# Three weight sums from VectorE to GpSimd, and a new order of turns, sums and writes around the fifth and sixth unit of a linear-attention and MLP kernel

## The chip, the core and the metric

The kernel runs on one core of a Trainium2 chip. The metric is the device time of one execution in microseconds. The core has TensorE (PE, with its weight loads shown as PEld), VectorE (DVE), ScalarE (ACT), GpSimd (POOL) and the DMA queues, most of which SyncE (SP) issues here. Each engine works through its own instructions in program order and waits on semaphores for the others.

## What is computed

The first half is a recurrence over 768 steps, for 4 batches and 8 heads of 48 channels; the second is an MLP with SiLU on its output.

```
for t in range(S):
    cur = einsum('bhd,bhe->bhde', u * k[t], v[t])
    y[t] = einsum('bhd,bhde->bhe', r[t], state + cur)
    state = w[t][..., None] * state + einsum('bhd,bhe->bhde', k[t], v[t])
x = y.transpose(0, 2, 1, 3).reshape(3072, 384)
h = x @ w_in                     # 384 -> 2048
out = (h * sigmoid(h)) @ w_out   # 2048 -> 384
```

Everything is float32.

## The kernel before

The work is cut into 12 units: 6 chunks of 128 time steps by 2 pairs of batches. The code counts them from 0, so the fourth, fifth, sixth and last unit are units 3, 4, 5 and 11. A unit has three parts, and the main loop (L1435) runs them staggered: its pass i does the attention of unit i (`mix(i)`), the second MLP layer of unit i-2 (`downs`) and the first MLP layer of unit i-1 (`ups`). `mix(i)` returns a list of groups, each a list of attention steps with a count: after a group's steps so many steps of the MLP are issued. This list is an order written out by hand, and since every engine keeps program order, it sets who runs before whom on each engine and on SP's DMA queue. Places in the text are indices into that list.

**Attention of a unit.** `turn` transposes raw w, k or r from tokens to channels (DVE, L361, two instructions, one for each batch). `product` (POOL, L410) builds the running products of w over 2, 4, 8, ... steps, levels 0 to 6. `grow_own`, `grow_keys` (POOL, L651 and L642) and `grow_queries`, `prepare` (DVE, L624 and L779) multiply these into keys and queries. `burst` (PE, L700) makes the scores of two levels, `keep_masked` (DVE, L718) and ACT (L800) keep the right blocks of them. The scores inside small blocks come another way: `block_bonus` (POOL, L493, steps 0 to 7) multiplies on untransposed data, `block_sum` (DVE, L530) reduces, `block_move` sends the sums through DRAM, `block_turn` (L563) and `block_write` (DVE, L569, one predicated copy for each half of the heads) put them into the score tile; units below 4 use `bonus_write` (L598) instead. At the end `y_state` (PE, L843 and L850) and `y_values` (L864) read the whole score tile.

**First MLP layer.** For units 0 to 2 it is a plain product (`up`, L1078). From unit 3 (`NFAST`) on, the layer is done as 20 products of weight combinations by combinations of x (`first_part`, PE at L1185), a bilinear scheme that saves multiplications. I call them by their numbers in `ORDER`: 20, 18, 14, 13, 2, 15, 4, 7, 19, 16, 1, 12, 9, 11, 3, 6, 10, 5, 8, 17. They accumulate in four PSUM banks A to D (`h1`, `h0`, `o1`, `o0`); ACT copies, SiLUs (L1209) and DVE joins (L1212) work on the banks in between. The combinations of x are DVE instructions (`sums_of_x`, steps 0 to 7, L1146 to L1166). The combinations of the weights are made once, 512 columns at a time, by `in_weight_sum` (L1124), during passes 3 and 4, on DVE or POOL; `weight_plan` names them (`q`, `n13`, `t`, `u1`, `u`, `q19`, `q9` and so on) and says what each reads and writes. Half of them overwrite blocks of `w_in_sb` that the plain products of unit 2 have read before.

**Second MLP layer.** It works the same way with 7 products (`quarter`, PE at L1328) of 192 columns. Quarters 2 to 5 use combinations of the SiLU outputs: `sums(i, m)` makes s1, s3, s2, s4 in this order on DVE (L1299) for m = 0 and 1. The seven results go through three places x, z, y in the banks `o0`, `h1`, `o1`: quarters 0, 2, 4 and 6 in x, 1 in z, 3 and 5 in y. A quarter may not go on in its place before the result that was there has been read: by ACT (L1333) after quarters 0, 2, 3 and 6, by DVE (L1336) after 1, 4 and 5. So quarter 6 waits for DVE's L1336 after quarter 4. Product 18 of the next first layer starts in bank `o1` and so waits for L1336 after quarter 5; product 17 is the last that uses `o0`.

In pass i the order on PE is: quarters of unit i-2, the first `burst`, products of unit i-1 with the second `burst` among them (between 11 and 3), `turn_apart`, `y_state`, `y_values`, `update`.

Of the kernel before, what the change touches and what calls it, by code (L numbers as in the profile page):

```python
# [38 lines left out]
def kernel(  # L39
# [921 lines left out]
    def mix(i):  # L961
# [12 lines left out]
        def turns(j):  # L974
            return [*at(j <= NPAIR, *both(turn, j, "w"), (product, j, 0)), *both(turn, j, "k")]

        def start(j):
            return [*at(j <= NPAIR, *products_of(j, *range(1, NL))), (grow_own, j, 1)]

# [6 lines left out]
        if i < NPAIR:  # L986
# [8 lines left out]
                      [(prepare, i, 5), (make_block_mask,), (bonus_spread, i)],  # L995
                      [(burst, i, 5), (keep_level, i, 5, 0), (keep_level, i, 6, 0), (go_on, i, 6), (bonus_write, i, (0,)), (keep_level, i, 5, 1), (keep_level, i, 6, 1), (bonus_write, i, (1,))], *end]
            groups = list(zip(groups, (1, 1, 0, 2, 1, 1, 1, 1, 1, 2, 2, 1, 1)))
        else:
            j = i - 1
            if i <= NPAIR:  # L1000
# [18 lines left out]
                          ([(block_write, i, 0), *at(i == NPAIR, *both(turn, i + 1, "w"))], 1),  # L1019
                          ([*end[0], *at(i == NPAIR, *products_of(i + 1, *range(NL)))], 2), (end[1], 0)]  # L1020
            else:
# [6 lines left out]
                groups = [([*both(turn, i, "r"), (grow_own, i, 0), (x_out, j, nc.sync), *loads("w", 0, 1)], 2),  # L1028
                          ([*at(j >= NPAIR, (add_update, j)), *start(i), *bonus_steps(i, 4), (x_in, j, nc.sync), *loads("w", 2, 3), (reverse_v, i)], 1),
                          ([*keys_2, *loads("k", 0, 1)], 1),  # L1030
                          ([*keys_3, (sums_of_x, j, 0, 1), *loads("k", 2)], 1),
                          ([(sums_of_x, j, 2), *bonus_steps(i, 6, 7), (sums_of_x, j, 3, 4, 5, 6), *loads("k", 3)], 2),
                          ([(burst, i, 3), *sum_steps(i, 3), (keep_level, i, 3), *sum_steps(i, 4)], 2),
                          ([(block_move, i, False), *at(ahead, (load_rk, i + 1, (0, 1)), (turn, i + 1, 0, "w"))], 1),
                          ([*loads("r", 0)], 1),
                          ([(block_move, i, True), *at(ahead, (turn, i + 1, 1, "w"), *products_of(i + 1, 0, 1, 2)), (keep_level, i, 4)], 2),
                          ([(go_on, i, 4), *at(ahead, *products_of(i + 1, 3, 4, 5, 6))], 1),
# [5 lines left out]
                          ([*loads("r", 3)], 1),  # L1043
                          ([(burst, i, 5), (keep_level, i, 5, 0), (keep_level, i, 6, 0), *at(ahead, *bonus_steps(i + 1, 0)), (go_on, i, 6), (block_turn, i), (block_write, i, 1)], 2),
                          ([(keep_level, i, 5, 1), (keep_level, i, 6, 1)], 1),
                          ([(block_write, i, 0)], 1),
                          ([*at(ahead, *bonus_steps(i + 1, 1, 2, 3)), ], 2),
# [238 lines left out]

    def sums(i, m):

# [8 lines left out]
        for out, one, two, op in ((s1, lower[1], upper[1], ALU.add), (s3, lower[0], lower[1], ALU.subtract),  # L1297
                                  (s2, s1, lower[0], ALU.subtract), (s4, upper[0], s2, ALU.subtract)):
            nc.vector.tensor_tensor(out=out, in0=one, in1=two, op=op)  # L1299
# [3 lines left out]
    def quarter(i, which):  # L1303
# [16 lines left out]
        if which in (0, 1, 3):  # L1320
            if i < NFAST - 1:
                pool, tag = (ps, "p_h") if place == "z" else (second[0], "p_o")
                sum_of[i, place] = pool.tile([128, DH], F32, name=tag, bufs=2)
            else:
                sum_of[i, place] = kept[{"x": "o0", "y": "o1", "z": "h1"}[place]][:, 0:DH]
        p = sum_of[i, place]
# [160 lines left out]
```

## Time and profile before

| | |
|---|---|
| median of 3 runs | 574.52 us (574.39 to 574.62) |
| the profiled execution | 573.2 us |
| its span, first to last instruction | 571.4 us |
| outside the span | 1.8 us |
| PE, DVE, POOL, ACT busy | 555.4, 481.7, 394.3, 270.8 us |
| granted TensorE clock | 1.0 in every slice |

A row of the timeline has the start, the duration, engine, line, operation, output and inputs, form and count; a bracket at its end is the idle time of the engine before the row and what ended it. Neighbouring instructions of one line are merged into a row with their count. Times are in microseconds from the span's start. The passes begin on PE with quarter 0: pass 4 at 169.97, pass 5 at 214.83, pass 6 at 260.57, pass 7 at 303.00, pass 11 at 471.39; the last quarters begin at 549.93.

### The profile page before, as it was taken

The numbers are of one execution on the slowest core, as the hardware profiler recorded it, in microseconds if no ns is written. First come the engines' busy times: TensorE is split into PE (matmuls) and PEld (weight loads), VectorE is DVE, ScalarE is ACT, GpSimd is POOL, SyncE is SP. The second block draws the span as 40 slices with busy tenths as digits, with TensorE's granted clock in tenths as the row PEclk, the third lists the DMA queues.
The fourth block names the chain that finished last, engine by engine and source line by source line (L and its number), as shares of the span: only waits on it lengthen the run. The fifth ranks groups of instructions, "written<-read, shape, count | busy, mean of one in ns | idle before, by whom it ended". The sixth has DMA issues, their size and how long they took to land.

```text
span 571.4 us, 18874 instructions
## 1 busy us (share of the span) xinstructions
PE 555.4 (97%) x7782; PEld 517.3 (91%) x7782; DVE 481.7 (84%) x748; ACT 270.8 (47%) x604; POOL 394.3 (69%) x447
## 2 busy tenths in 40 slices
PE   8989999999999999799999999999999999999997
PEld 8767776698889889799999999999999999999997
DVE  7979798998999999989989989989989889782250
ACT  5679695442451273274274274274274272271320
POOL 5998778537879999696696696696696696600000
PEclk9999999999999999999999999999999999999999
DMA  9955876345355365364465454465555452102000
GB/s 224 311 106 148 238 224 128 47 69 108 89 87 96 77 112 96 60 129 89 93 109 91 101 103 91 94 108 93 109 88 95 104 96 61 38 5 56 29 9 21
DMA packets 206485, 57.59 MB, mean 101 GB/s; under 512 B 186048, under 2 KB 198208, under 8 KB 206400
## 3 DMA queue, kind: packets, MB, share of 16 engines
q1 hardware_dynamic: 203712, 54.23, 46.1%
q10 hardware_dynamic: 2688, 2.16, 1.5%
q8 instruction: 61, 1.00, 0.8%
q14 instruction: 24, 0.20, 0.1%
HBM read 47.14 MB, written 9.18 MB: 99 GB/s over the span
## 4 chain that ended last, share of the span: by engine, by line
PE 73%; DVE 11%; POOL 4%; DMA 4%; SPq 3%; issue 3%; ACT 1%; DVEq 0%; POOLq 0%
PE p_o L1328 25%; PE p_o L1185 15%; PE p_h L1185 10%; PE p_h L1078 5%; PE p_h L1328 4%; PE p_m L1267 4%; PE p_sc L700 2%; PE p_m L864 2%; SPq L127 2%; POOL tk L642 2%; DVE score L718 2%; PE p_m L843 1%; DVE tr L624 1%; PE p_m L700 1%; DMA tokens_w<-in_w_dram 1%
## 5 line engine op out<-in xcount | busy, mean ns | idle before, releaser
L642 POOL TENSOR_TENSOR tk<-tk,tw 128x256 f32<-128x256 f32 x112 | 92.6, 846 | 7.8 <-DVE tw L410 3.8
L1328 PE MATMUL p_o<-own,temps 128*128 128x192 f32 x528 | 88.1, 327 | 0.2 <-DVE temps L1299 0.2
L1328 PEld LDWEIGHTS p_o<-own,temps 128*128 128x128 f32 x528 | 86.0, 190 | 0.5 <-DVE temps L1299 0.5
L1185 PE MATMUL p_o<-xt,w_in_sb 128*64 128x128 f32 x1152 | 72.1, 273 | 0.7 <-POOL w_in_sb L1124 0.7
L1078 PE MATMUL p_h<-xt,w_in_sb 128*128 128x256 f32 x288 | 66.1, 384 | 1.7 <-POOL w_in_sb L260 1.6
L1185 PEld LDWEIGHTS p_o<-xt,w_in_sb 128*64 128x64 f32 x1152 | 64.7, 137 | 0.9 <-POOL w_in_sb L1124 0.9
L1328 PE MATMUL p_o<-w_out_sb,gt 128*128 128x192 f32 x340 | 60.1, 330 | 4.1 <-DVE ob L1336 3.4
L1078 PEld LDWEIGHTS p_h<-xt,w_in_sb 128*128 128x128 f32 x288 | 53.6, 190 | 9.9 <-POOL w_in_sb L260 2.4
L410 POOL TENSOR_TENSOR tw<-tw 128x256 f32<-128x256 f32 (+6 forms) x71 | 39.6, 558 | 33.0 <-DVE tw L361 29.4
L1328 PEld LDWEIGHTS p_o<-w_out_sb,gt 128*128 128x128 f32 x340 | 55.2, 190 | 5.6 <-DVE ob L1336 4.0
L493 POOL TENSOR_TENSOR ruk<-tokens_rk 128x384 f32<-128x384 f32 x48 | 53.0, 1124 | 4.4 <-DMA tokens_rk<-in_k_dram 4.4
L624 DVE TENSOR_TENSOR tr<-tr,tw 128x512 f32<-128x512 f32 x57 | 51.6, 905 | 0.7
L1333 ACT COPY partial<-p_o 128x192 f32<-128x192 f32 x33 | 10.5, 319 | 77.2 <-PE p_o L1328 77.2
L1299 DVE TENSOR_TENSOR temps<-gt 128x512 f32<-128x512 f32 (+1 forms) x48 | 44.3, 961 | 0.0
L651 POOL TENSOR_TENSOR tk<-tk,tw 128x256 f32<-128x256 f32 x32 | 24.7, 806 | 27.5 <-DVE tk L361 27.5
L612 ACT COPY tk<-tk 128x256 f32<-128x256 f32 x52 | 20.9, 402 | 36.6 <-POOL tk L642 29.4
L1209 ACT ACTIVATE gt<-p_o 128x512 f32<-128x512 f32 x45 | 26.1, 602 | 25.1 <-PE p_o L1185 25.1
L1333 ACT COPY ob<-p_o 128x192 f32<-128x192 f32 x11 | 3.5, 319 | 61.2 <-PE p_o L1328 61.2
L718 DVE COPY_PREDICATED score<-mask,p_sc 128x512 f32<-128x512 int8 x42 | 31.2, 799 | 0.9 <-PE p_sc L700 0.8
L1328 PE MATMUL p_o<-w_out_sb,temps 128*128 128x192 f32 x176 | 30.4, 326 | 0.0
L1328 PE MATMUL p_h<-w_out_sb,gt 128*128 128x192 f32 x168 | 29.1, 326 | 0.0
L493 POOL TENSOR_TENSOR spare<-tokens_rk 128x384 f32<-128x384 f32 x24 | 28.6, 1204 | 0.6
(247 smaller groups left out, 1315.3 us busy)
## 6 DMA issues: line engine op xcount, KB each, us to landing
w_out_sb<-in_moe_w_in_dram SPq DMA_DIRECT2D x6, 768.0 KB, 7.5
turned<-yt SPq DMA_DIRECT2D x18, 192.0 KB, 2.6
xt<-turned SPq DMA_DIRECT2D x9, 384.0 KB, 3.4
w_out_sb<-in_moe_w_out_dram SPq DMA_DIRECT2D x4, 768.0 KB, 5.4
own<-in_moe_w_out_dram SPq DMA_DIRECT2D x4, 768.0 KB, 5.9
tokens_w<-in_w_dram SPq DMA_DIRECT2D x8, 384.0 KB, 4.4
tokens_rk<-in_r_dram SPq DMA_DIRECT2D x7, 384.0 KB, 4.7
tokens_rk<-in_k_dram SPq DMA_DIRECT2D x7, 384.0 KB, 5.9
```

What stands on the lines that cost most here:

```text
L410: engine.tensor_tensor(out=up, in0=t[:, :, 0::2], in1=t[:, :, 1::2], op=ALU.mult)
L493: mul = lambda out, one, two: nc.gpsimd.tensor_tensor(out=out, in0=one, in1=two, op=ALU.mult)
L624: nc.vector.tensor_tensor(out=odd, in0=odd, in1=tw[i][l][:, :, 0::2][:, :, :, None].to_broadcast([128, Q, L >> (l + 1), c]), op=ALU.mult)
L642: nc.gpsimd.tensor_tensor(out=out, in0=have, in1=odd_products(i, l, b, *blocks), op=ALU.mult)
L651: nc.gpsimd.tensor_tensor(out=have, in0=have, in1=odd_products(i, l, b, [2, NP * ni]), op=ALU.mult)
L718: nc.vector.copy_predicated(out=dst, mask=masks[l][:, :, None].to_broadcast([128, NB, NP, ni, c]), data=sc[e].rearrange("p (b q) (i c) -> ...
L1078: nc.tensor.matmul(p_h[:, a, :], lhsT=w_in_sb[:, c, f * 128:(f + 1) * 128], rhs=xt[i][:, c, :], start=(a == 0 and c == 0), stop=(a == 1 an ...
L1185: nc.tensor.matmul(p[h:h + PD, q, :], lhsT=left[:, f:f + PD], rhs=right, start=first and q == 0, stop=q == 3, skip_group_check=True)
L1209: nc.scalar.activation(out=g(f, t), in_=have, func=AF.Silu)
L1267: nc.tensor.matmul(po[i, b], lhsT=gt[i, f // 2][:, f % 2, b * L:(b + 1) * L], rhs=w_out_sb[:, f, :], start=(f == 0), stop=(f == FC - 1))
L1299: nc.vector.tensor_tensor(out=out, in0=one, in1=two, op=op)
L1328: nc.tensor.matmul(p, lhsT=left(f), rhs=right[:, f, :], start=which in (0, 1, 3) and f == 0, stop=f == FH - 1, skip_group_check=True)
```

## The change

No instruction is added or taken away; instructions change their engine or their place in the order, and one PSUM place changes its bank.

1. Weight sums. `q`, `n13`, `t` (POOL) go from place 11 of pass 3 to place 10, ahead of `block_bonus` 0 to 3 of unit 4. `u1`, `u`, `q19`, which DVE made in pass 4 (places 5 and 7), are made by POOL at place 11 of pass 3, behind `block_bonus` 0 to 3.
2. Turns. The two turns of w of unit 4 go from the end of pass 3 to place 10 of pass 3, ahead of the `bonus_write`s. In pass 5 the first turn of w of unit 6 goes from place 6 to place 8, next to the second.
3. Products of w. Levels 1 to 6 of unit 5 go from the end of pass 4 (place 19) into pass 5 (place 1, behind `grow_own` level 0). Level 0 stays.
4. Sums. Of `sums(3, 1)` only s1 and s2 stay at the end of pass 4; s3 and s4 go into pass 5, behind the turns of r. `sums_of_x` 0 and 1 go from place 3 to place 4, behind quarter 4 with its L1336, in passes 5 and 11.
5. Writes. In pass 5 `block_write` 1 goes from place 16 to place 18, directly ahead of `block_write` 0 and behind product 10 with its join.
6. The last unit's quarter 0 (and with it 2, 4 and 6) accumulates in a bank of `p_sc` instead of `o0`.

```diff
         def turns(j):
-            return [*at(j <= NPAIR, *both(turn, j, "w"), (product, j, 0)), *both(turn, j, "k")]
+            return [*at(j <= NPAIR, (product, j, 0)), *both(turn, j, "k")]
         def start(j):
-            return [*at(j <= NPAIR, *products_of(j, *range(1, NL))), (grow_own, j, 1)]
+            return [*at(j <= NPAIR + 1, *products_of(j, *range(1, NL))), (grow_own, j, 1)]
...
-    ... (go_on, i, 6), (bonus_write, i, (0,)), ...
+    ... (go_on, i, 6), *at(i == NPAIR - 1, *both(turn, i + 1, "w")), (bonus_write, i, (0,)), ...
...
-    ([*end[0], *at(i == NPAIR, *products_of(i + 1, *range(NL)))], 2), (end[1], 0)]
+    ([*end[0], *at(i == NPAIR, *products_of(i + 1, 0))], 2), (end[1], 0)]
...
-    groups = [([*both(turn, i, "r"), (grow_own, i, 0), ...
+    groups = [([*both(turn, i, "r"), *at(j == NPAIR, (sums, j - 1, 1, (1, 3))), (grow_own, i, 0), ...
...
-    ([*keys_3, (sums_of_x, j, 0, 1), *loads("k", 2)], 1),
-    ([(sums_of_x, j, 2), *bonus_steps(i, 6, 7), ...
+    ([*keys_3, *at(NPAIR + 1 < i < len(units) - 1, (sums_of_x, j, 0, 1)), *loads("k", 2)], 1),
+    ([*at(i in (NPAIR + 1, len(units) - 1), (sums_of_x, j, 0, 1)), (sums_of_x, j, 2), *bonus_steps(i, 6, 7), ...
...
-    ([(block_move, i, False), *at(ahead, (load_rk, i + 1, (0, 1)), (turn, i + 1, 0, "w"))], 1),
+    ([(block_move, i, False), *at(ahead, (load_rk, i + 1, (0, 1))), *at(ahead and i > NPAIR + 1, (turn, i + 1, 0, "w"))], 1),
...
-    ([(block_move, i, True), *at(ahead, (turn, i + 1, 1, "w"), ...
+    ([(block_move, i, True), *at(i == NPAIR + 1, (turn, i + 1, 0, "w")), *at(ahead, (turn, i + 1, 1, "w"), ...
...
-    ... (block_turn, i), (block_write, i, 1)], 2),
+    ... (block_turn, i), *at(i > NPAIR + 1, (block_write, i, 1))], 2),
...
-    ([(block_write, i, 0)], 1),
+    ([*at(i == NPAIR + 1, (block_write, i, 1)), (block_write, i, 0)], 1),
...
-    def sums(i, m):
+    def sums(i, m, which=range(4)):
...
-    sum_of[i, place] = kept[...][:, 0:DH]
+    sum_of[i, place] = bank("p_sc", DH) if i == len(units) - 1 and which == 0 else kept[...][:, 0:DH]
...
-    made[-1].append((sums, i, 1))
+    made[-1].append((sums, i, 1, range(4) if i > NFAST else (0, 2)))
...
-    (8, nc.vector, ("q12a", "q12")), (11, nc.gpsimd, ("q", "n13", "t"))):
+    (8, nc.vector, ("q12a", "q12")), (10, nc.gpsimd, ("q", "n13", "t")), (11, nc.gpsimd, ("u1", "u", "q19"))):
...
-    for place, engine, names in ((5, nc.vector, ("u1", "u")), (7, nc.vector, ("q19",)), (5, nc.gpsimd, ("q7",)),
+    for place, engine, names in ((5, nc.gpsimd, ("q7",)),
```

More of the change, by code (lines that the diff above doesn't have):

```diff
@@ L995, in mix @@
                       [(prepare, i, 5), (make_block_mask,), (bonus_spread, i)],
-                      [(burst, i, 5), (keep_level, i, 5, 0), (keep_level, i, 6, 0), (go_on, i, 6), (bonus_write, i, (0,)), (keep_level, i, 5, 1), (keep_level, i, 6, 1), (bonus_write, i, (1,))], *end]
+                      [(burst, i, 5), (keep_level, i, 5, 0), (keep_level, i, 6, 0), (go_on, i, 6), *at(i == NPAIR - 1, *both(turn, i + 1, "w")), (bonus_write, i, (0,)), (keep_level, i, 5, 1), (keep_level, i, 6, 1), (bonus_write, i, (1,))], *end]
             groups = list(zip(groups, (1, 1, 0, 2, 1, 1, 1, 1, 1, 2, 2, 1, 1)))
@@ L1043, in mix @@
                           ([*loads("r", 3)], 1),
-                          ([(burst, i, 5), (keep_level, i, 5, 0), (keep_level, i, 6, 0), *at(ahead, *bonus_steps(i + 1, 0)), (go_on, i, 6), (block_turn, i), (block_write, i, 1)], 2),
+                          ([(burst, i, 5), (keep_level, i, 5, 0), (keep_level, i, 6, 0), *at(ahead, *bonus_steps(i + 1, 0)), (go_on, i, 6), (block_turn, i), *at(i > NPAIR + 1, (block_write, i, 1))], 2),
                           ([(keep_level, i, 5, 1), (keep_level, i, 6, 1)], 1),
-                          ([(block_write, i, 0)], 1),
+                          ([*at(i == NPAIR + 1, (block_write, i, 1)), (block_write, i, 0)], 1),
                           ([*at(ahead, *bonus_steps(i + 1, 1, 2, 3)), ], 2),
@@ L1296, in sums @@
             s1, s2, s3, s4 = (quarters[:, x, 2 * m:2 * m + 2, :] for x in range(4))
-        for out, one, two, op in ((s1, lower[1], upper[1], ALU.add), (s3, lower[0], lower[1], ALU.subtract),
-                                  (s2, s1, lower[0], ALU.subtract), (s4, upper[0], s2, ALU.subtract)):
+        made = ((s1, lower[1], upper[1], ALU.add), (s3, lower[0], lower[1], ALU.subtract),
+                (s2, s1, lower[0], ALU.subtract), (s4, upper[0], s2, ALU.subtract))
+        for out, one, two, op in (made[x] for x in which):
             nc.vector.tensor_tensor(out=out, in0=one, in1=two, op=op)
@@ L1324, in quarter @@
             else:
-                sum_of[i, place] = kept[{"x": "o0", "y": "o1", "z": "h1"}[place]][:, 0:DH]
+                sum_of[i, place] = bank("p_sc", DH) if i == len(units) - 1 and which == 0 else kept[{"x": "o0", "y": "o1", "z": "h1"}[place]][:, 0:DH]
         p = sum_of[i, place]
```

6 lines of the change are left out of this document (3 added, 3 removed).

## The prediction

> **What bounds the kernel now.** I read the passes first, as stretches of the span: length, then busy time of PE, its weight loads, DVE, ACT and POOL.
>
> ```profile
> 169.97:214.83 44.86, 43.04 (x690) 41.37 (x688) 43.72 (x67) 18.38 (x43) 43.92 (x46) 1.00 0.51 94
> 214.83:260.57 45.74, 42.77 (x693) 41.59 (x689) 42.43 (x62) 20.57 (x52) 39.85 (x46) 1.00 0.50 92
> 260.57:303.00 42.43, 42.43 (x689) 41.54 (x689) 39.03 (x61) 20.50 (x52) 32.80 (x37) 1.00 0.52 97
> 430.30:471.39 41.09, 41.09 (x641) 40.23 (x641) 37.68 (x60) 19.05 (x49) 31.85 (x37) 1.00 0.53 100
> 471.39:513.22 41.83, 41.36 (x641) 40.20 (x641) 36.31 (x60) 17.85 (x42) 20.57 (x25) 1.00 0.15 35
> ```
>
> Pass 6 is filled by PE: 42.43 of 42.43 us, at full clock. Pass 4 takes 2.43 us more and pass 5 3.31 us more; pass 11 takes 0.74 us more than pass 10, which has the same work on PE. In pass 4 DVE and POOL are busy for all but 1 us. So the most there is to win is 2.43 + 3.31 + 0.74, and something at the end. The timeline of PE shows the places (start, duration, ..., idle before it and its releaser).
>
> ```profile
> 196.21 1.09 PE L1185 MATMUL p_o<-gt,in_sum 128*64 128x128 f32 x16 [0.96 <-DVE p_o L1212]
> 202.36 1.09 PE L1185 MATMUL p_o<-xt,w_in_sb 128*64 128x128 f32 x16 [0.69 <-POOL w_in_sb L1124]
> 227.93 2.76 PE L1328 MATMUL p_o<-w_out_sb,temps 128*128 128x192 f32 x16
> 233.66 2.87 PE L1328 MATMUL p_o<-w_out_sb,gt 128*128 128x192 f32 x16 [2.97 <-DVE ob L1336]
> ```
>
> The first is product 4, waiting for the join after 13, which DVE does late; the second is product 9, waiting for its weights `q9` from POOL; the last is quarter 6 in pass 5, waiting for DVE to read quarter 4's result. That one wait is nearly all that pass 5 loses.
>
> **Part by part.** *The sums of x behind the read of quarter 4* (change 4).
>
> ```profile
> 231.69 0.80 DVE L1146 TENSOR_TENSOR xt<-xt 128x256 f32<-128x256 f32 x1
> 233.25 0.36 DVE L1336 TENSOR_TENSOR ob<-p_o,partial 128x192 f32<-128x192 f32 x1
> ```
>
> DVE works through its order up to this read; `sums_of_x` 0 and 1 take it from 231.69 to 233.25, so L1336 comes 1.56 us earlier without them. s3 and s4 of `sums(3, 1)` change places with the turns, all ahead of L1336: no gain there. `product` 1 to 6 of unit 5 keep their sum on POOL, which waits for the turn of k between them. I count both at nothing. In pass 11 the same move of 1.56 us is more than the wait: the 0.74 us go.
>
> *When DVE comes to pass 5.*
>
> ```profile
> 204.13 0.70 DVE L1212 TENSOR_TENSOR p_o<-p_h,gt 128x512 f32<-128x512 f32 x1 [0.69 <-ACT gt L1209]
> ```
>
> Here DVE stands still behind ACT's SiLU of product 9, so it starts towards pass 5 from where `q9` lets PE go. Taking `u1`, `u`, `q19` and a turn (169.81, below) off DVE in pass 4 removes the 0.96 us at product 4, but PE then only reaches product 9 earlier, and the wait for `q9` grows by as much. What counts is POOL, and what the weight sums do to it in pass 3.
>
> ```profile
> 154.30 1.19 POOL L642 TENSOR_TENSOR tk<-tk,tw 128x256 f32<-128x256 f32 x2
> 159.88 2.29 POOL L493 TENSOR_TENSOR ruk<-tokens_rk 128x384 f32<-128x384 f32 x2 [4.40 <-DMA tokens_rk<-in_k_dram]
> 166.73 1.47 POOL L1124 TENSOR_TENSOR raw<-w_in_sb 128x512 f32<-128x512 f32 x1
> 169.68 1.34 POOL L1124 TENSOR_TENSOR raw<-raw,w_in_sb 128x512 f32<-128x512 f32 x1
> ```
>
> ```profile
> 155.58 0.68 DVE L624 TENSOR_TENSOR tr<-tr,tw 128x512 f32<-128x512 f32 x1
> 157.08 1.30 DVE L598 COPY_PREDICATED score<-own_mask,both_b 128x1024 f32<-128x1024 int8 x1 [0.82 <-ACT score L800]
> 158.91 1.30 DVE L598 COPY_PREDICATED score<-own_mask,both_b 128x1024 f32<-128x1024 int8 x1 [0.53 <-ACT score L800]
> 169.81 1.29 DVE L361 STREAM_TRANSPOSE tw<-raw 128x512 f32<-128x512 f32 x2
> ```
>
> POOL pauses from 155.49 to 159.88, 4.39 us, for a DMA. `q`, `n13`, `t` (from 166.73, three until 171.02) go into it; `u1`, `u`, `q19` have the same size and take their old place. The two turns of w fill DVE's idle 0.82 and 0.53 us; no DMA changes its place on SP, and the loads of unit 5's w, which wait for these turns, can only go earlier. But DVE and POOL hold each other up:
>
> ```profile
> 251.67 2.68 POOL L642 TENSOR_TENSOR tk<-tk,diag 128x256 f32<-128x256 f32 x2
> ```
>
> ```profile
> 252.44 1.47 DVE L569 COPY_PREDICATED score<-spare 128x1024 f32<-128x1024 int8 x1
> ```
>
> ```profile
> 193.28 1.72 POOL L1124 TENSOR_TENSOR w_in_sb<-w_in_sb,raw 128x512 f32<-128x512 f32 x1
> 194.96 1.71 POOL L1124 TENSOR_TENSOR w_in_sb<-raw,w_in_sb 128x512 f32<-128x512 f32 x1
> 196.75 1.28 POOL L1124 TENSOR_TENSOR w_in_sb<-in_sum,w_in_sb 128x512 f32<-128x512 f32 x1
> ```
>
> ```profile
> 191.47 0.98 DVE L1124 TENSOR_TENSOR w_in_sb<-w_in_sb 128x512 f32<-128x512 f32 x1
> 192.48 1.38 DVE L1124 TENSOR_TENSOR w_in_sb<-raw,w_in_sb 128x512 f32<-128x512 f32 x1
> 194.65 0.90 DVE L1124 TENSOR_TENSOR w_in_sb<-w_in_sb 128x512 f32<-128x512 f32 x1
> ```
>
> A weight sum takes POOL 1.28 us alone and 1.72 or 1.71 us beside one on DVE: such a DVE instruction costs POOL about 0.43 us. Two L642 take 1.19 us alone (154.30) and 2.68 us beside a predicated copy of 1024 elements and an L624: 1.49 us, of which I give 0.43 to L624 and 1.06 to the copy. The pause must then hold 3 x 1.28 for the sums, 0.43 for L624 and 2 x 1.06 for the copies: 6.39 us, 2.0 too many. Before, the second copy already reached 0.33 us (158.91 + 1.30 against 159.88) into the instruction behind the pause, so POOL leaves it 1.67 us later. It gets back 3 x 0.43 = 1.29 us in pass 4, where DVE's three sums are gone. From 159.88 to `q9` POOL has hardly a pause, so `q9` comes 1.67 - 1.29 = 0.4 us later. The ends: 1.3 us earlier if nothing overflows, 1.7 us later if nothing comes back. I take 0.4 because both terms have rows of the same instructions.
>
> The Trainium skill ("SBUF — State Buffer", Who interferes with whom) says that a DVE instruction with two SBUF inputs and a GpSimd instruction that reads SBUF exclude each other on a shared port, whoever comes second being blocked to the end. By whole durations the pause would overflow by 3 x 1.28 + 0.68 + 2 x 1.30 - 4.39 = 2.7 us; the row 251.67 shows the blocking, though 1.72 against 1.28 shows less than a whole instruction of it.
>
> So quarter 6 in pass 5 starts 1.56 - 0.4 = **1.2 us** earlier (ends: 2.9 and -0.1; the wait itself allows 3).
>
> *What is late next in pass 5.*
>
> ```profile
> 236.71 0.34 DVE L1336 TENSOR_TENSOR temps<-p_o,partial 128x192 f32<-128x192 f32 x1
> ```
>
> ```profile
> 238.48 1.04 PE L1185 MATMUL p_o<-xt,w_in_sb 128*64 128x128 f32 x16
> ```
>
> Product 18 needs the bank that this L1336 reads. From the end of the L1336 at 233.25 (233.61) DVE needs 3.44 us to the end of this one, and 1.56 more with the two sums between: 5.0. PE, from quarter 6, is there after 238.48 - 233.66 = 4.82 us. A wait of **0.2 us** comes in (0 to 0.5). The turn of w of unit 6 that moves two places back (0.65 us, half of the row at 169.81) holds up POOL's `product`s for the second burst by at most itself; POOL waits for both turns anyway, so I count nothing.
>
> *The write behind product 10's join.*
>
> ```profile
> 253.98 0.70 DVE L1212 TENSOR_TENSOR p_o<-gt,p_h 128x512 f32<-128x512 f32 x1
> 254.59 1.92 DVE L569 COPY_PREDICATED score<-spare 128x1024 f32<-128x1024 int8 x1
> ```
>
> ```profile
> 257.95 0.22 PE L850 MATMUL p_m<-score,vt 64*48 64x64 f32 x1
> ```
>
> ```profile
> 275.58 0.36 DVE L1336 TENSOR_TENSOR ob<-p_o,partial 128x192 f32<-128x192 f32 x1
> ```
>
> ```profile
> 276.20 2.76 PE L1328 MATMUL p_o<-w_out_sb,gt 128*128 128x192 f32 x16
> ```
>
> Before, the copy at 252.44 filled DVE's time until product 10 was done; now DVE idles there (`block_turn` is done before 252.44, the join begins at 253.98), and both copies come behind the join: from 254.59, at 1.47 to 1.92 us each, until 257.5 to 258.4. L850, which reads both halves, stood at 257.95: a wait of 0 to 0.4 us. Queued behind the copies are the sums for pass 6, up to its L1336, which had 276.20 - 275.94 = 0.26 us to spare; DVE comes 1.0 to 1.9 us later, so up to 1.6 us could be lost. But POOL runs ahead in DVE's idle time and leaves the later sums undisturbed. I take **0.3 us** in all (0 to 1.6).
>
> *The last quarter's bank.*
>
> ```profile
> 548.41 0.61 ACT L1209 ACTIVATE gt<-p_o 128x512 f32<-128x512 f32 x1
> ```
>
> ```profile
> 549.93 2.87 PE L1328 MATMUL p_o<-w_out_sb,gt 128*128 128x192 f32 x16 [0.70 <-ACT gt L1209]
> ```
>
> Quarter 0 waits for the last SiLU, which reads `o0`. Its own inputs are done with the SiLU before, at 549.02, while PE is still at product 17. In another bank it starts at about 549.1: **0.8 us** (0.7 to 0.9), and nothing later depends on another engine.
>
> *Sum:* 1.2 - 0.2 - 0.3 + 0.74 + 0.8 = 2.2 us. The span goes from 571.4 to 569.2, the profiled execution from 573.2 to 571.0, the median from 574.52 (1.3 above the profiled execution) to **572.3**.
>
> **The rivals.** *More: the pause takes it all.* If POOL's sums and DVE's copies fit between each other, `q9` comes 1.3 us earlier and quarter 6 2.9 us: 2.9 - 0.2 - 0.3 + 1.54 = 3.9 us, 570.6. For it speaks that DVE waits for ACT in the pause and could use other gaps; against it the 2.68 us row.
>
> *No change: passes 4 and 5 only change their waits.* If POOL's 1.67 us are not won back, and the writes cost pass 6 0.8 us, there remain -0.1 - 0.2 - 0.8 + 1.54 = 0.4 us, 574.1. For it speaks that POOL is busy 43.92 of 44.86 us in pass 4. The Trainium skill ("Perfetto Trace Analysis", Optimizing Scalar/DVE Operations) holds that moving work between these two engines might not help, for the same port; no run here shows it yet.
>
> *Slower: unit 2's plain products wait for `u1` to `q19`.*
>
> ```profile
> 155.22 8.04 PE L1078 MATMUL p_h<-xt,w_in_sb 128*128 128x256 f32 x36
> 190.71 1.04 PE L1185 MATMUL p_o<-xt,w_in_sb 128*64 128x128 f32 x16
> ```
>
> The last two of unit 2's `up`s stand behind these sums in the program and read other columns of `w_in_sb`. Were the wait kept for the tile and not for the columns, the seventh `up` (the last third of the row at 155.22, at about 160.5) would wait for the end of `q19` near 172: 11 us, of which pass 4's waits absorb 2, so 574.5 + 9 - 1.5 = 582. Against it: product 18 read `w_in_sb` at 190.71, before `u1`, which stands ahead of it in the program, was written at 191.47. It decides as soon as POOL's sums end after 160.5.
>
> **How the numbers follow.** Forecast (gain 1.2 to 3.2): 0.45. More: 0.22. No change: 0.25. Slower: 0.08. What a measurement of this kernel can tell from no change is about 0.2%, 1.15 us: so faster 0.67, same 0.25, slower 0.08. The range reaches from the first rival's 570.6 with the writes and product 18 at nothing and the tail at its best (569.9) to no gain at all, 574.5; it leaves out the slower case and a little of the others.
>
> **What would show it.** Right: no idle before product 4; product 9 still waiting for `q9`, by about 2 us, at 202 to 203; quarter 6 of pass 5 waiting 1 to 2 us for L1336; L493 behind the pause starting near 161.5; pass 11 at 41.1 us; the last quarter 0 right behind product 17. Wrong: product 9 before 201.5 (the pause sufficed), L1336 of pass 6 ending after PE is ready (the writes), or an idle PE before an `up` near 160 (the slower rival).

## The result and the profile after

| | before | after |
|---|---|---|
| median of 6 runs each | 574.38 us (573.81 to 574.62) | 572.20 us (571.82 to 572.64) |
| profiled execution | 573.2 us | 571.82 us |
| its span | 571.4 us | 570.0 us |

The ratio is 0.9963 with a 95% interval of 0.995 to 0.9976: 0.37% faster, 2.2 us by the medians and 1.4 us by the two profiled executions. The forecast was 572.3.

The total by the medians is what I said, but the steps are not. First the passes of the kernel after: length, then busy time of PE, its weight loads, DVE, ACT and POOL. In this kernel and in those made from it, the lines from the old L1299 on are shifted by one: the sums are L1300, the quarters L1329, DVE's read L1337.

```profile
169.67:214.52 44.85, 42.82 (x690) 41.40 (x688) 42.09 (x64) 18.39 (x43) 43.99 (x47) 1.00 0.49 92
214.52:260.68 46.16, 43.62 (x693) 41.80 (x689) 39.67 (x63) 20.33 (x52) 38.00 (x46) 1.00 0.50 91
471.50:512.59 41.09, 41.09 (x642) 40.23 (x641) 36.63 (x61) 17.87 (x42) 20.57 (x25) 1.00 0.15 35
```

Pass 4 is as long as before (44.86), pass 5 is 0.4 us longer (45.74), pass 6 is the same (42.42 us), pass 11 is 0.74 us shorter (41.83). Now the places on PE:

```profile
178.45 6.12 PE L1329 MATMUL p_o<-own,temps 128*128 128x192 f32 x36 [1.47 <-DVE temps L1300]
...
196.08 1.04 PE L1185 MATMUL p_o<-gt,in_sum 128*64 128x128 f32 x16
...
202.05 1.09 PE L1185 MATMUL p_o<-xt,w_in_sb 128*64 128x128 f32 x16 [0.56 <-POOL w_in_sb L1124]
...
231.77 2.87 PE L1329 MATMUL p_o<-w_out_sb,gt 128*128 128x192 f32 x16 [1.38 <-DVE ob L1337]
...
249.33 0.68 PE L700 MATMUL p_m<-tr,tk 48*64 48x64 f32 x28 [0.23 <-POOL tk L642]
...
257.97 0.31 PE L850 MATMUL p_m<-score,vt 64*48 64x64 f32 x2 [0.88 <-DMA raw<-in_r_dram]
...
548.54 2.87 PE L1329 MATMUL p_sc<-w_out_sb,gt 128*128 128x192 f32 x16
```

Product 4's wait is gone (196.08), but a wait of 1.47 us for the sums of unit 2 has come in ahead of it (178.45; before, this wait was 0.17 us), so pass 4 wins nothing. Quarter 6 of pass 5 waits 1.38 us where it waited 2.97; it stands 1.9 us earlier than before (231.77 against 233.66), 1.6 us counted from the start of pass 4. L850 then stands at 257.97, the place it had before (257.95): whatever was won up to quarter 6 is lost again behind it, in the second burst and at L850. The last quarter 0 follows product 17 with no wait.

POOL's timeline shows what became of the pause:

```profile
153.89 1.19 POOL L642 TENSOR_TENSOR tk<-tk,tw 128x256 f32<-128x256 f32 x2
155.03 1.27 POOL L1124 TENSOR_TENSOR raw<-w_in_sb 128x512 f32<-128x512 f32 x1
156.38 1.61 POOL L1124 TENSOR_TENSOR raw<-in_sum,raw 128x512 f32<-128x512 f32 x1
158.07 2.30 POOL L1124 TENSOR_TENSOR raw<-raw,w_in_sb 128x512 f32<-128x512 f32 x1
160.32 3.17 POOL L493 TENSOR_TENSOR ruk<-tokens_rk 128x384 f32<-128x384 f32 x2
...
191.91 1.98 POOL L493 TENSOR_TENSOR ruk<-tokens_rk 128x384 f32<-128x384 f32 x2
193.84 1.27 POOL L1124 TENSOR_TENSOR w_in_sb<-w_in_sb,raw 128x512 f32<-128x512 f32 x1
195.07 1.28 POOL L1124 TENSOR_TENSOR w_in_sb<-raw,w_in_sb 128x512 f32<-128x512 f32 x1
...
242.40 2.70 POOL L410 TENSOR_TENSOR tw<-tw 128x512 f32<-128x512 f32 x3 [3.00 <-DVE tw L361]
```

The three sums take 1.27, 1.61 and 2.30 us, against 1.28 for the shortest before. The two L493 behind the pause end at 163.49 instead of 162.17. In pass 4 the sums that took 1.72 and 1.71 us take 1.27 and 1.28. The last row is POOL's wait for the turns of w of unit 6, one of which was moved two places back. The kernel before waits there too:

```profile
242.77 2.69 POOL L410 TENSOR_TENSOR tw<-tw 128x512 f32<-128x512 f32 x3 [4.15 <-DVE tw L361]
```

Before, POOL went on 9.11 us after the start of quarter 6, and now it does so 10.63 us after it: in the pass these products come 1.5 us later. And DVE's side in the kernel after:

```profile
155.17 1.68 DVE L624 TENSOR_TENSOR tr<-tr,tw 128x512 f32<-128x512 f32 x1
156.77 1.29 DVE L361 STREAM_TRANSPOSE tw<-raw 128x512 f32<-128x512 f32 x2
158.00 3.54 DVE L598 COPY_PREDICATED score<-own_mask,both_b 128x1024 f32<-128x1024 int8 x2
...
252.89 0.69 DVE L1212 TENSOR_TENSOR p_o<-gt,p_h 128x512 f32<-128x512 f32 x1 [1.77 <-PE p_h L1185]
254.30 3.61 DVE L569 COPY_PREDICATED score<-spare 128x1024 f32<-128x1024 int8 x2 [0.72 <-ACT score L800]
```

In the pause L624 takes 1.68 us instead of 0.68, and the two copies 3.54 instead of 1.30 each. The ends look as if the two engines took turns: L624 ends 0.55 us after POOL's first sum, the second sum 1.14 us after L624, the second copy 1.17 us after the third sum, so that most of each one's own time lies behind the end of the other.

DVE comes out of the pause late, but that alone is not the 1.47 us wait at 178.45. The two turns of w that were taken out of its way behind the pause give most of it back: at the turns of k DVE is only 0.37 us late, counted from the start of pass 4 (171.10 in a pass from 169.67, before 171.03 in a pass from 169.97). The rest comes behind these turns. Before:

```profile
172.22 1.02 DVE L1299 TENSOR_TENSOR temps<-gt 128x256 f32<-128x256 f32 x2
```

And after, with what POOL does beside it:

```profile
172.32 1.92 DVE L1300 TENSOR_TENSOR temps<-gt 128x256 f32<-128x256 f32 x2
172.26 1.04 POOL L410 TENSOR_TENSOR tw<-tw 128x512 f32<-128x512 f32 x1
```

POOL's product L410 ended before (171.18 to 172.22) just where DVE began these two sums. Now POOL is late, L410 stands beside them, and they take 0.9 us longer. Together with the 0.4 us that is the 1.3 us by which the wait grew. This is read from the rows; no run isolates it.

Behind product 10's join the two writes take 3.61 us and end at 257.91; L850 starts 0.06 us later.

### The profile page after: what moved, and what is told of

Its sections match the earlier page's. It is cut to its first block, busy times and chain, and to the rows that moved or that the text cites. A ratio compares the mean times of both kernels' runs of the same rounds, so it can differ in the third digit from the quotient of the medians.

```text
span 570.0 us, 18875 instructions
## 1 busy us (share of the span) xinstructions
PE 556.4 (98%) x7782; PEld 517.9 (91%) x7782; DVE 477.6 (84%) x745; ACT 270.6 (47%) x604; POOL 396.8 (70%) x450
## 4 chain that ended last, share of the span: by engine, by line
PE 76%; DVE 9%; POOL 8%; issue 2%; DMA 2%; ACT 1%; SPq 1%; DVEq 0%; POOLq 0%
PE p_o L1329 24%; PE p_o L1185 15%; PE p_h L1185 10%; PE p_h L1078 6%; PE p_h L1329 4%; PE p_m L1267 4%; POOL tk L642 2%; PE p_sc L700 2%; PE p_m L864 2%; DVE temps L1300 2%; PE p_sc L1329 2%; DVE score L718 2%; PE p_m L843 1%; PE p_m L700 1%; DMA raw<-in_r_dram 1%
## 5 line engine op out<-in xcount | busy, mean ns | idle before, releaser
L1329 PE MATMUL p_o<-own,temps 128*128 128x192 f32 x496 | 82.9, 326 | 1.5 <-DVE temps L1300 1.5
L1329 PEld LDWEIGHTS p_o<-own,temps 128*128 128x128 f32 x496 | 80.8, 190 | 1.8 <-DVE temps L1300 1.8
L1078 PE MATMUL p_h<-xt,w_in_sb 128*128 128x256 f32 x288 | 67.7, 391 | 0.8 <-POOL w_in_sb L260 0.8
L410 POOL TENSOR_TENSOR tw<-tw 128x256 f32<-128x256 f32 (+6 forms) x71 | 38.8, 546 | 33.0 <-DVE tw L361 29.6
L1329 PE MATMUL p_o<-w_out_sb,gt 128*128 128x192 f32 x308 | 54.4, 329 | 1.4 <-DVE ob L1337 1.4
L493 POOL TENSOR_TENSOR ruk<-tokens_rk 128x384 f32<-128x384 f32 x48 | 54.3, 1151 | 0.0
L1329 PEld LDWEIGHTS p_o<-w_out_sb,gt 128*128 128x128 f32 x308 | 50.1, 190 | 2.3 <-DVE ob L1337 1.7
L624 DVE TENSOR_TENSOR tr<-tr,tw 128x512 f32<-128x512 f32 x57 | 51.1, 896 | 0.6
L1300 DVE TENSOR_TENSOR temps<-gt 128x512 f32<-128x512 f32 (+1 forms) x48 | 44.6, 965 | 0.0
L718 DVE COPY_PREDICATED score<-mask,p_sc 128x512 f32<-128x512 int8 x42 | 31.2, 798 | 0.8 <-PE p_sc L700 0.6
L1329 PE MATMUL p_o<-w_out_sb,temps 128*128 128x192 f32 x176 | 30.4, 326 | 0.0
L493 POOL TENSOR_TENSOR spare<-tokens_rk 128x384 f32<-128x384 f32 x24 | 29.1, 1228 | 0.6
L1329 PE MATMUL p_h<-w_out_sb,gt 128*128 128x192 f32 x168 | 29.1, 326 | 0.0
L1329 PEld LDWEIGHTS p_o<-w_out_sb,temps 128*128 128x128 f32 x176 | 28.9, 190 | 0.0
```

The source lines that it names most:

```text
L410: engine.tensor_tensor(out=up, in0=t[:, :, 0::2], in1=t[:, :, 1::2], op=ALU.mult)
L493: mul = lambda out, one, two: nc.gpsimd.tensor_tensor(out=out, in0=one, in1=two, op=ALU.mult)
L624: nc.vector.tensor_tensor(out=odd, in0=odd, in1=tw[i][l][:, :, 0::2][:, :, :, None].to_broadcast([128, Q, L >> (l + 1), c]), op=ALU.mult)
L718: nc.vector.copy_predicated(out=dst, mask=masks[l][:, :, None].to_broadcast([128, NB, NP, ni, c]), data=sc[e].rearrange("p (b q) (i c) -> ...
L1078: nc.tensor.matmul(p_h[:, a, :], lhsT=w_in_sb[:, c, f * 128:(f + 1) * 128], rhs=xt[i][:, c, :], start=(a == 0 and c == 0), stop=(a == 1 an ...
L1329: nc.tensor.matmul(p, lhsT=left(f), rhs=right[:, f, :], start=which in (0, 1, 3) and f == 0, stop=f == FH - 1, skip_group_check=True)
```

## The experiments

My theory after this reading: the gain comes from three small moves (the sums of x in pass 5, those in pass 11, the last bank), the move of the weight sums brings nothing, and the two writes behind product 10's join cost 1 us. Each ratio below is against runs of the kernel before on the same chip.

**The writes back in their place** (against the kernel after):

```diff
-... (block_turn, i), *at(i > NPAIR + 1, (block_write, i, 1))], 2),
+... (block_turn, i), (block_write, i, 1)], 2),
...
-([*at(i == NPAIR + 1, (block_write, i, 1)), (block_write, i, 0)], 1),
+([(block_write, i, 0)], 1),
```

> The changed kernel with part 5 alone undone: in pass 5 block_write 1 stands at place 16 again, ahead of product 10's join. Theory (the write costs): in the changed kernel L850 starts 0.88 us late because both predicated copies come behind the join and end at 257.91; with one copy back in DVE's idle 1.77 us this wait goes, pass 5 takes 1.2 us less than its 46.16 us (about 45.0), and the time is 572.2 - 1.2 = 571.0 us, ratio to the kernel before about 0.994. Rival (the releaser that the profile names, a DMA of raw r, is the true one): the wait stays, 572.2 us, pass 5 at 46.1 us. Second rival: DVE comes late to product 10's join and product 17 waits instead, at most 0.6 us, so 571.6 us.

Measured 570.76 us, 0.9944 (0.9926 to 0.9961). The waits in the kernel after, between 245 and 262, name two releasers for L850, one for the matmul and one for its weight load:

```profile
PEld p_m L850 <- DVE score L569: 1.1, 1, 1.1
...
PE p_m L850 <- DMA raw<-in_r_dram: 0.9, 1, 0.9
```

With the writes back, the timeline of PE has:

```profile
249.55 0.68 PE L700 MATMUL p_m<-tr,tk 48*64 48x64 f32 x28 [0.22 <-POOL tk L642]
...
256.18 1.13 PE L843 MATMUL p_m<-tr,state 48*48 48x128 f32 x32
257.09 0.22 PE L850 MATMUL p_m<-score,vt 64*48 64x64 f32 x1
```

L850 follows L843 at once, and pass 5 takes 44.89 us instead of 46.16. So the write was the cause, the weight load's row named it, and the DMA in the matmul's row had nothing to do with it. The edit cost 1.3 us; without it the change gives 0.56%. The small wait in the second burst is still there.

**The turn of w of unit 6 back at its place too** (against the last):

```diff
-... *at(ahead and i > NPAIR + 1, (turn, i + 1, 0, "w"))], 1),
+... *at(ahead, (turn, i + 1, 0, "w"))], 1),
...
-([(block_move, i, True), *at(i == NPAIR + 1, (turn, i + 1, 0, "w")), *at(ahead, ...
+([(block_move, i, True), *at(ahead, ...
```

> As the run before, and the first turn of w of unit 6 is at place 6 of pass 5 again, ahead of the join of product 13. Theory (the turn's place costs): POOL's products for unit 6 start 0.65 us earlier, the second burst of pass 5 and product 3 behind it lose less than the 0.8 us that they lose in the changed kernel: another 0.5 us less, 570.5 us, pass 5 at about 44.5 us. Rival (POOL is late for another reason, because levels 1 to 6 of unit 5's products stand behind the turn of k): no difference to the run before, 571.0 us.

Measured 571.07 us, 0.9949 (0.9931 to 0.9966); pass 5 took 45.0 us. The wait in the burst is gone, but a new one stands ahead of it:

```profile
241.76 1.09 PE L1185 MATMUL p_o<-gt,in_sum 128*64 128x128 f32 x16 [0.65 <-DVE p_o L1212]
```

The turn, back at its earlier place, delays DVE's join ahead of product 4. I had expected another 0.5 us less, and there is no gain: putting the turn back takes the burst's wait away and brings another as long.

**The ends alone** (against the kernel before): the last unit's quarter 0 in its own bank, and the sums of x 0 and 1 behind quarter 4 in pass 11.

```diff
-sum_of[i, place] = kept[...][:, 0:DH]
+sum_of[i, place] = bank("p_sc", DH) if i == len(units) - 1 and which == 0 else kept[...][:, 0:DH]
...
-([*keys_3, (sums_of_x, j, 0, 1), *loads("k", 2)], 1),
-([(sums_of_x, j, 2), *bonus_steps(i, 6, 7), ...
+([*keys_3, *at(i < len(units) - 1, (sums_of_x, j, 0, 1)), *loads("k", 2)], 1),
+([*at(i == len(units) - 1, (sums_of_x, j, 0, 1)), (sums_of_x, j, 2), *bonus_steps(i, 6, 7), ...
```

> The kernel before with two small parts alone: the last unit's quarter 0 in its own bank, and sums_of_x 0 and 1 behind quarter 4 in pass 11 (not in pass 5). Theory (nearly all of the gain is here): 0.74 + 0.76 = 1.5 us less, 572.9 us, ratio 0.9974, passes 4 and 5 as before (44.86 and 45.74 us). Rival (the gain comes from weight sums, turns and pass 5, and the two ends are hidden elsewhere): under 0.5 us, 574 us or more.

Measured 572.87 us, 0.9969 (0.9951 to 0.9986). Passes 4 and 5 are as before (44.75 and 45.66), pass 11 is 41.09 us. The two ends bring 0.3% by themselves.

**The sums of x in pass 5 alone** (the same two lines as above, with `i != NPAIR + 1` and `i == NPAIR + 1`):

> The kernel before with one part alone: sums_of_x 0 and 1 behind quarter 4 in pass 5. Theory (this move alone brings quarter 6 forward): quarter 6 waits 1.5 us less than 2.97 us; product 18 may wait 0.2 us; the time is 574.4 - 1.3 = 573.1 us, pass 5 at 44.4 us. Rival (DVE's relief in pass 4 brings quarter 6 forward): quarter 6 as before, 574.4 us. Second rival (POOL is behind and the second burst takes it back): quarter 6 earlier, pass 5 still near 45.5 us, 574.1 us.

Measured 571.57 us, 0.9959 (0.9944 to 0.9975), 1.5 us less time than I expected. The passes, columns as above, and quarter 6:

```profile
169.49:214.34 44.85, 43.03 (x689) 41.37 (x687) 43.71 (x67) 18.37 (x43) 43.91 (x46) 1.00 0.49 92
214.34:258.74 44.40, 42.85 (x692) 41.50 (x688) 42.83 (x62) 20.50 (x52) 39.68 (x46) 1.00 0.48 92
```

```profile
231.76 2.87 PE L1328 MATMUL p_o<-w_out_sb,gt 128*128 128x192 f32 x16 [1.55 <-DVE ob L1336]
```

Pass 5 is 1.3 us shorter and pass 4 the same, as expected, and the span is 1.6 us shorter. The medians differ by 2.6 us; the last section has a possible reason for the rest. Quarter 6 comes 62.27 us after the start of pass 4. In the whole change it is 62.10 and before it was 63.69: this one move gives nearly all of it.

**The weight sums alone** (against the kernel before: the two lists of weight sums of change 1 and the turns of w of unit 4 of change 2, nothing else):

> The kernel before with part 1 (the weight sums) and the turns of w of unit 4 alone. Theory (q9 on POOL holds PE in pass 4 whatever DVE has to do, and the pause's overflow of 1.7 us takes back what POOL wins): pass 4 within 0.3 us of 44.86, product 9 still waiting for q9, quarter 6 of pass 5 still waiting near 3 us, 574.3 us, no difference from the kernel before. Rival (DVE relieved of 3.3 us of sums comes earlier to pass 5): quarter 6 waits 1.5 us less, 572.8 us.

Measured 574.35 us, 1.0004 (0.9993 to 1.0015): no change. PE's waits in passes 4 and 5 have moved:

```profile
179.00 6.12 PE L1328 MATMUL p_o<-own,temps 128*128 128x192 f32 x36 [1.46 <-DVE temps L1299]
...
202.59 1.09 PE L1185 MATMUL p_o<-xt,w_in_sb 128*64 128x128 f32 x16 [0.55 <-POOL w_in_sb L1124]
...
233.94 2.87 PE L1328 MATMUL p_o<-w_out_sb,gt 128*128 128x192 f32 x16 [3.02 <-DVE ob L1336]
```

Pass 4 starts at 170.22 here and takes 44.84 us, so nothing is won in it, and quarter 6 comes after 63.72 us, against 63.69. The headline of the change, three sums from one engine to the other, is worth nothing by itself. Here the trace agrees with the Trainium skill ("Perfetto Trace Analysis", Optimizing Scalar/DVE Operations), by which moving work between these two engines might not help.

**The weight sums not in the pause** (against the kernel after): all six sums on POOL at place 11.

```diff
-... (10, nc.gpsimd, ("q", "n13", "t")), (11, nc.gpsimd, ("u1", "u", "q19"))):
+... (11, nc.gpsimd, ("q", "n13", "t")), (11, nc.gpsimd, ("u1", "u", "q19"))):
```

> The changed kernel with q, n13 and t at place 11 of pass 3 again, ahead of u1, u and q19, so that POOL's pause stays empty and six sums follow block_bonus 3. Theory (the pause is worth what it holds, less what DVE's copies take of it): POOL gets three sums of 1.33 us more into pass 4 and loses the 1.7 us by which the pause overflows, so q9 comes 2.3 us later, product 9 of pass 4 waits about 2.9 us, pass 4 takes 47.2 us, and the time is 572.2 + 2.3 = 574.5 us. Rival (moving sums between engines that hold each other up is worth nothing, wherever they stand): 572.2 us, pass 4 within 0.3 us of 44.85.

Measured 574.94 us, 1.0009 (1.0 to 1.0017): 2.7 us slower than the kernel after, so the pause does hold work that would otherwise delay pass 4. The time is near the 574.5 us that I expected, but by another way. PE waits for DVE's sums of unit 2, and not at all for `q9`:

```profile
180.41 7.78 PE L1329 MATMUL p_o<-own,temps 128*128 128x192 f32 x36 [3.17 <-DVE temps L1300]
...
234.67 2.87 PE L1329 MATMUL p_o<-w_out_sb,gt 128*128 128x192 f32 x16 [0.71 <-DVE ob L1337]
```

DVE's timeline has the steps between:

```profile
170.86 2.91 DVE L1300 TENSOR_TENSOR temps<-gt 128x256 f32<-128x256 f32 x2
177.22 1.12 DVE L932 TENSOR_TENSOR state<-p_sc,state 48x384 f32<-48x384 f32 x2 [0.86 <-POOL state L914]
```

The two sums that took 1.02 us in the kernel before take 2.91 us beside POOL's weight sums, which run until 174.90. Then DVE stands 0.86 us behind POOL's update of the state, which is queued behind the six sums.

And the 36 matmuls behind the wait take 7.78 us instead of 6.12. The windows of this kernel show why (the number behind POOL's busy time and count is the granted clock):

```profile
177.00:180.40 3.40, 0.23 (x2) 0.00 (x0) 3.10 (x6) 0.00 (x0) 3.24 (x6) 1.00 0.46 58
180.40:182.00 1.60, 1.59 (x5) 1.60 (x6) 1.60 (x3) 0.00 (x0) 1.36 (x5) 0.50 0.37 43
182.00:184.00 2.00, 2.00 (x9) 2.00 (x8) 1.97 (x4) 0.32 (x1) 2.00 (x4) 0.54 0.40 51
```

After the wait of 3.17 us the granted clock is 0.50 for some 3.3 us, which costs PE 1.66 us (7.78 - 6.12); from 184 on it is 1.00 again. How much of the 2.7 us that is, the run can't say: behind it quarter 6 still waits for DVE, for 0.71 us.

**The products of w back at the end of pass 4** (the kernel after with the writes back, and levels 1 to 6 of unit 5 where they were):

```diff
-... *at(j <= NPAIR + 1, *products_of(j, *range(1, NL))), ...
+... *at(j <= NPAIR, *products_of(j, *range(1, NL))), ...
...
-... *at(i == NPAIR, *products_of(i + 1, 0))], 2), ...
+... *at(i == NPAIR, *products_of(i + 1, *range(NL)))], 2), ...
```

> The changed kernel with two parts undone: block_write 1 at place 16, as in the first run, and unit 5's products of levels 1 to 6 back at the end of pass 4. Theory (POOL is late in pass 5 because it idles 1.97 us for the turn of k with the products still to do): no idle there, block_sum 3 no longer waits 1.6 us for POOL, and the second burst loses its 0.2 us wait and what goes with it: pass 5 at 44.4 us in place of the first run's 44.9, 570.3 us. Rival (the turn of w two places back is what delays the second burst): as the first run, 570.8 us, the wait at the second burst is still there.

Measured 570.80 us, 0.9935 (0.9923 to 0.9947). Passes 4 and 5 take 44.85 and 44.51 us: 0.4 less than with the writes back alone, and the burst has no wait.

```profile
232.34 2.87 PE L1329 MATMUL p_o<-w_out_sb,gt 128*128 128x192 f32 x16 [1.67 <-DVE ob L1337]
...
249.26 0.65 PE L700 MATMUL p_m<-tr,tk 48*64 48x64 f32 x32
```

So the products that were moved into pass 5 made POOL late for the burst. The median is the rival's number, since 0.4 us can't be told in the medians; the theory holds by the passes and the wait alone.

**The three small moves together**, on the kernel before: the sums of x behind quarter 4 in passes 5 and 11, and the last bank. Nothing of the weight sums, turns, products and writes.

> The kernel before with three small moves alone: sums_of_x 0 and 1 behind quarter 4 in passes 5 and 11, and the last unit's quarter 0 in its own bank. Theory (these are all of the gain, the weight sums, turns, products and writes of the change give nothing): 1.34 + 0.74 + 0.76 = 2.8 us less, pass 5 at 44.4 us, pass 11 at 41.1 us, 574.1 - 2.8 = 571.3 us or a little less, and not slower than the first run's 570.8 by more than 0.5. Rival (the weight sums on POOL are worth at least 1 us of it): 572.3 us.

Measured 570.34 us, 0.9935 (0.9921 to 0.9948), 1.0 us less time than I expected. This beats both kernels: the intervals of this ratio and of the whole change (0.995 to 0.9976) don't touch.

Three further kernels on top of it go for the waits that are left in pass 4, at products 4 and 9 (0.99 and 0.69 us in the kernel with the three moves).

**The order of pass 4 alone:** `q5` and `q9` earlier on POOL, `q19` later on DVE.

```diff
-... (7, nc.vector, ("q19",)), (5, nc.gpsimd, ("q7",)),
-    (8, nc.gpsimd, ("q8", "q1")), (9, nc.gpsimd, ("q5", "q9")), ...
+... (5, nc.gpsimd, ("q7",)),
+    (8, nc.gpsimd, ("q8", "q1", "q5", "q9")), ...
...
+        if i == NFAST + 1:
+            groups[8][0].insert(0, (in_weight_sum, nc.vector, "q19"))
```

> The run before and two moves in pass 4, no sum changes its engine: q19 goes from ahead of the join of product 13 to behind it (start of place 8, DVE), and q5 and q9 go ahead of go_on of level 4 on POOL (place 8). Theory (pass 4 is bound by where the join and q9 stand in the two orders, not by how much DVE has to do): the waits of 0.96 us at product 4 and 0.69 us at product 9 go, pass 4 takes 43.2 us in place of 44.86, 1.6 us less than the run before, 569.7 us. Rival (POOL and DVE are full, so something else waits as long): product 19 for q19, or the second burst for the keys that now come 2.6 us later: within 0.5 us of the run before.

Measured 570.10 us, 0.9929 (0.9917 to 0.9942), not to be told from the last. The two waits are gone and two others are there:

```profile
199.81 1.16 PE L1185 MATMUL p_h<-spare,raw 128*64 128x128 f32 x16 [0.40 <-DVE p_h L1212]
...
202.41 1.09 PE L1185 MATMUL p_h<-spare,w_in_sb 128*64 128x128 f32 x16 [0.57 <-DVE p_h L1212]
...
231.74 2.87 PE L1328 MATMUL p_o<-w_out_sb,gt 128*128 128x192 f32 x16 [1.78 <-DVE ob L1336]
```

Pass 4 is 44.48 us, but quarter 6 of pass 5 comes where it came (62.22 us after the start of pass 4, against 62.15).

**The weight sums and the early `q9` together** (the three moves, the edits of the run with the weight sums alone, and `q5`, `q9` at place 8):

> The run with three small moves (sums of x in passes 5 and 11, the last bank) and with it part 1, the turns of w of unit 4, and q5 and q9 ahead of go_on of level 4. Theory (DVE and q9 bind pass 4 together, so that moving q9 alone or relieving DVE alone gives nothing, and both together do): no wait at products 4, 9, 11 and 12, pass 4 at 44.0 us in place of 44.86, its wait for the sums of unit 2 near 178 (1.5 us) stays, and the time is 570.3 - 0.9 = 569.4 us. Rival (no gain from the weight sums in any order): 570.3 us.

Measured 570.42 us, 0.9934 (0.9922 to 0.9946): no gain either. Products 4 and 9 don't wait, as expected, but pass 4 takes 44.50 us instead of 44.0, and pass 5 takes 44.86 us instead of the 44.37 of the three moves alone.

**The turns of w of unit 5 early as well** (from place 18 to place 6 of pass 4):

> The run before, and the turns of w of unit 5 go from the end of pass 4 (place 18) to place 6, into the 1.2 us in which DVE idles ahead of the join of product 13. Theory (quarter 6 of pass 5 waits for DVE, which is late by what it does between product 11 and there): DVE comes 1.28 us earlier to pass 5, quarter 6 waits at most 0.3 us in place of 1.5, and the time is 569.4 - 1.2 = 568.2 us. Rival (POOL, whose bonus steps and products run through to pass 5, holds up DVE's sums there instead): 569.0 us or more, block_sum or prepare in pass 5 waiting for POOL.

Measured 571.02 us, 0.9943 (0.993 to 0.9956): nothing is won. DVE is held up, as the rival has it, but for 0.93 us by a DMA of the block sums that it had not waited for, and not by POOL.

So one number stands through all these kernels: with the sums of x moved, quarter 6 of pass 5 comes 62.1 to 62.4 us after the start of pass 4, whatever is done in pass 4 (the one exception is the run without the pause, 64.75). How that happens is best seen between the three moves alone and the same with the weight sums. Windows of the first, the columns as above (the pause, the start of pass 4's sums, the whole stretch up to quarter 6):

```profile
155.00:160.00 5.00, 5.00 (x25) 4.38 (x24) 3.64 (x5) 3.71 (x12) 1.57 (x1) 1.00 0.77 169
175.00:180.00 5.00, 4.96 (x31) 4.67 (x31) 4.90 (x10) 0.32 (x1) 4.61 (x10) 1.00 0.71 128
169.45:231.60 62.15, 58.91 (x786) 56.95 (x784) 60.76 (x94) 23.58 (x58) 60.55 (x65) 1.00 0.49 91
```

and of the second:

```profile
155.00:160.00 5.00, 5.00 (x25) 4.41 (x24) 5.00 (x6) 3.76 (x12) 4.84 (x3) 1.00 0.81 172
175.00:180.00 5.00, 3.41 (x21) 3.11 (x20) 4.92 (x10) 0.32 (x1) 4.61 (x10) 1.00 0.65 128
169.38:231.57 62.19, 58.94 (x786) 57.09 (x784) 58.81 (x91) 23.23 (x58) 60.60 (x65) 1.00 0.50 91
```

The pause is really filled: POOL is busy for 4.84 us of these 5 instead of 1.57. But DVE had only 1.36 us of idle time there, and has none now: L624 and the two copies take longer, and it leaves the pause late. At the turns of k 0.6 us of this is left, and the two sums behind them take 1.92 us instead of 1.03, as in the kernel after. From 175 to 180 PE stands still for 1.6 us for DVE's sums. In the whole stretch DVE is busy 2.0 us less (58.81 against 60.76) and the end is the same: what its queue was relieved of, it waits for PE instead, which it has itself made late. This last step is read from the rows; no run isolates it.

## Why the prediction was right, and where it was not

The forecast of 2.2 us agrees with the medians, but part of that is luck. My sum went from the profiled execution of 573.2 to one of 571.0 us, and I carried the 1.3 us from the profiled execution to the median over as it was. The profiled execution came to 571.82 us, so it gained 1.4 us. Of this, 0.30 us lie ahead of pass 4, where the change has no part (`grow_keys` ahead of the pause starts at 153.89 instead of 154.30). Then come 0.0 in pass 4, 0.4 lost in pass 5, 0.74 won in pass 11 and 0.76 in the tail: 1.1 us, half of what I had added up. The other 0.8 us of the medians is in no term of mine; the last section has a possible reason.

- *The pause overflows by 1.67 us*: 1.73. From the start of `grow_keys` to the end of the two L493 behind the pause it was 7.87 us (154.30 to 162.17) and is 9.60 (153.89 to 163.49). The size holds, the parts do not: I charged the three sums 2.55 us of contention, and they took 1.34 us more than 3 x 1.28; the two L493 behind them took 0.88 us more.
- *A fixed price, 0.43 us for a weight sum on DVE and 1.06 us for a copy*: the two rows that I read fit better with the rest of DVE's instruction. The sum at 193.28 begins 0.58 us before DVE's ends (192.48 + 1.38), the one at 194.96 0.59 us before it (194.65 + 0.90). So the price depends on where the two meet, and that my 1.72 us was less than a whole instruction says nothing against a block to the end.
- *POOL gets 1.29 us back*: 1.31 (0.43, 0.45 and 0.43 on an L493 pair and two sums). `q9` came 0.4 us sooner than I said, at 32.38 us after the start of the pass against 32.39: no gain and no loss. Product 9 waits 0.56 us and not 2, because PE had already lost 1.47 us ahead of it.
- *DVE in pass 4*: here a step was missing. I charged POOL for the contention of the pause, but not DVE. It came out of the pause late, then met POOL's late L410 in its sums of unit 2 (0.9 us), and PE waits 1.47 us for it at 178.45. Product 4's wait did go.
- *Quarter 6 comes 1.2 us earlier*: 1.59, from the start of pass 4. The run with that one move has 1.42 of it, the weight sums alone nothing.
- *Product 18 waits 0.2 us*: not at all.
- *The second burst, counted at nothing*: 0.8 us lost from quarter 6 to product 3 (18.17 us against 17.36). I had bounded the turn by 0.65 us and counted the moved products as free, since POOL waits for the turn of k anyway. The products were not free (0.4 us of pass 5, by the run with them back).
- *The write behind product 10's join, 0.3 us (0 to 1.6)*: 1.2 to 1.3 us. This is the mis-sized term. I let the copies begin at 254.59 and end by 258.4 with L850 at its old time 257.95; but L850 should by then have been earlier by all that was won in the pass, so a copy that ends at 257.91 takes that gain away. The end was within my bounds, the place that it was to be compared with was not.
- *Pass 11, 0.74 us; the last quarter's bank, 0.8 us*: 0.74 and 0.76.

The rival that there is no change, with passes 4 and 5 only trading their waits, is what these two passes did; the total is another because the two ends brought 1.5 us and the medians 0.8 us that the profiled executions don't have. The slower rival (a wait kept for the whole tile) did not show: no matmul of unit 2's products waits near 160.

## What to carry to other kernels

Where two engines that hold each other up are both busy for 97% of a stretch, work moved from one to the other, or into a pause of one beside the other's work, comes back as another wait; ask of each move what it takes from both. What helped here were moves that take work out of the way of one instruction that PE waits for (two sums behind a read, a bank of its own). And a gain in the middle of a pass must be carried to its end: each later instruction has to be earlier by the gain, or it is the new bound.

## What was unexpected of the hardware

- Predicated copies and GpSimd work beside them cost both sides: POOL's sums took up to 2.30 us instead of 1.28, and the copies 3.54 us for two instead of 2 x 1.30. In the second place of the change two copies took 3.61 us. Copies that read PSUM did not: in the kernel before two L718 from 196.93 take 1.34 us, and the weight sum beside them (196.75) 1.28.
- A wait of PE can halve its granted clock, and the length of that wait alone does not tell whether it will. A wait of 3.17 us did so for some 3.3 us (1.66 us lost), while waits of 2.97 us (before, ahead of quarter 6) and of 3.02 us (the weight sums alone) left the clock at 1.00 in the profiled executions. But in the kernel after a wait of 1.53 us, early in the kernel, did it too:

```profile
37.76 1.03 PE L700 MATMUL p_sc<-tr,tk 48*64 48x64 f32 x32 [1.53 <-POOL tk L666]
38.72 7.13 PE L1078 MATMUL p_h<-xt,w_in_sb 128*128 128x256 f32 x24
```

  From 39.5 to 42.5 the granted clock is 0.50. In the kernel before the same 24 matmuls follow a wait of 1.57 us and take 5.45 us at 1.00. The Trainium skill ("TensorE: Matmul & The Clock Gate", HAM oscillation — how this bites in real kernels) puts the limit of such a gap at about 3.4 us; these traces do not keep to it.
- The wait of 2.97 us ahead of quarter 6 may well have had such a price in most executions, though not in the profiled one. Of the 55 executions of the kernel before that were timed beside the experiments, 18 have a mean granted clock of 0.999 or 1.0 and take at most 573.60 us; the other 37 have 0.997 or less and take at least 573.86 us, by the medians of the two groups 1.1 us more. The two other kernels that keep this wait split in the same way: the ends alone (at most 572.01 us, at least 572.64) and the weight sums alone (573.58 and 574.22). With the sums of x moved in pass 5, which cuts the wait to 1.55 us, there is no such split (571.43 to 572.26 and 571.06 to 571.99 us). That would be the 0.8 us by which the medians fell more than the profiled executions. The clock of an execution is one mean over all of it, so where it dropped is not shown.
- A wait of PE that the matmul's row puts down to a DMA was one for DVE, named only by the row of the weight load ahead of it.
